# Order of TensorE's work in a chunk-attention loop: where the transposes of xr and the rank products stand

## The chip, the cores and the metric

One core of one Trainium2 chip runs the kernel. The metric is the device time of one execution in microseconds (us). The time before is the median of 3 runs, 677.48 us, the runs lying from 676.41 to 678.26 us.

## What is computed

Two blocks follow each other. The first is attention in chunks of 64 rows, without any link between chunks; the second routes each of the 4608 resulting rows (512 wide) to one of 8 experts by a cosine, and runs that expert's two-layer MLP.

```python
# q, k, v: (8, 8, 576, 64) float32, chunk = 64
scores = scale * q_c @ k_c.T            # 64x64 for each batch, head and chunk
scores = scores - max(scores)
attn = exp(scores); attn = attn / (sum(attn) + 1e-9)
x = (attn @ v_c)  -> rows of all heads: (4608, 512)
xn = x / (norm(x) + 1e-6); en = expert_emb / (norm(expert_emb) + 1e-6)
logits = xn @ en.T / tau                # 8 experts
e = argmax(logits); gate = softmax(logits)[e]
out = gate * (relu(x @ w1[e]) @ w2[e])  # w1: 8x512x1024, w2: 8x1024x512
```

## The kernel before

The 4608 rows are cut into NT = 36 tiles of 128 rows; one tile holds two chunks of all 8 heads. The loop of line 1024, `for t in range(-3, NT + 3)`, is a software pipeline over the tiles, and the order in which it calls its helpers is the order of each engine's queue: the schedule is written by hand (`tc.manual_schedule()`), nothing reorders it. A pass of the loop is called a turn here. In turn t the kernel works on several tiles at once:

- `turn_a(t)` (line 633) transposes the weights a of tile t, four 128x128 transposes on TensorE (L637) into a PSUM tile `tr`, and ScalarE copies them out as aT (L639).
- `turn_qk(t + 3)` (line 590) transposes k and then q of the tile three ahead (L595, four transposes each); ScalarE copies k out (L598), VectorE copies q out (L600). The loads of tile t + 7 (`load_qk`, GpSimd's queue) stand behind it.
- `logits(b)` (line 689), once in four turns, multiplies the transposed rows of a batch of RB = 4 tiles with the experts (L695); ScalarE copies the result (L703). `copy_logits(b)` (line 708) transposes it back on TensorE (L710), and VectorE copies it (L712).
- `scores(t + 2)` (line 603) issues sixteen 64x64 matmuls (L611); VectorE takes the maximum of them (mx, L619) and subtracts it (a, L621). `weights(t + 2)` (line 629) is ScalarE's exp (L631), later in the turn.
- `turn_x(t - 1)` (line 676) transposes the finished rows xr of the tile before (L680); ScalarE copies them out as xT (L682) and sums their squares (L685).
- `values(t)` (line 642) issues sixteen 64x65 matmuls with v (L651); VectorE divides by the sums of the weights: rs (L659), its reciprocal (L660), and the product that writes xr (L662). v of the next batch entry is loaded behind it (`load_v`, SyncE's queue, L584).
- `pick(b)` (line 716), late in the turn in which the logits come, finds each row's expert with five small VectorE instructions (L724 to L728, the last writes eqb_all). One turn later `place(b)` (line 732) counts ranks with five or more small bf16 matmuls (L737, L738, L746), the "rank products", and four VectorE instructions (L762 to L771) make the destinations. `put` scatters one tile a turn to DRAM on GpSimd's queue (L800).

All `tr` tiles come from one PSUM pool with three buffers, used in the order a, k, q, xr, a, and so on, so that each waits for the copy-out of the one three before. The scores have one PSUM buffer and the values have one (`ps_s` and `ps_v`, `bufs=1`).

Turns 33 to 38 are the way out: `early_parts` (line 1013) puts the first matmuls of the expert block there. Behind the loop, groups of 64 rows run through their expert's two layers (L342, L413 and others) until the end.

The loop's head before is (line 1024 on, loads and loops at the way out left out):

```python
turn_a(t); count_early(); turn_qk(t + 3); logits; [turn_x(t - 1) if t == NT]
early_parts(t, 0); scores(t + 2); copy_logits; place
[turn_x(t - 1) if t - 1 < NT - 1]; values(t); load_v
weights(t + 2); pick; put; early_parts(t, 1)
```

Of the kernel before, what the change touches and what calls it, by code (L numbers as in the profile page):

```python
# [25 lines left out]
def kernel(  # L26
# [19 lines left out]
    NT = N // P  # L46
# [77 lines left out]
    def load_first(buf, rows):  # L124

        for s in range(2):
            e = (0, E - 1)[s]
            nc.sync.dma_start(out=whole(buf[s]), in_=rows[:, e : e + 1, :], max_dma_last_dim=4096)
# [317 lines left out]
    with (  # L446
# [132 lines left out]
        def load_v(b, c0=0, c1=NCB, eng=nc.sync):  # L579

            t = v_sb[b % 2]
            for h in range(H):
                r0 = CH * (h % 2)
                eng.dma_start(  # L584
                    out=t[r0 : r0 + CH, h // 2, c0:c1, 0:Dh],
                    in_=v[b, h].rearrange("(c k) d -> k c d", k=CH)[:, c0:c1],
                )
            v_t[b] = t

        def turn_qk(t):  # L590
            for nm in ("kx", "qx"):
                a = qk_t.pop((nm, t))
                ps = ps_t.tile([P, NPAIR, P], FP32, tag="tr", name="tr")
                for i in range(NPAIR):
                    nc.tensor.transpose(ps[:, i], a[:, i * P : i * P + P], ident)  # L595
                x = wk.tile([P, NPAIR, P], FP32, tag=nm + "T", name=nm + "T")
                if nm == "kx":
                    nc.scalar.copy(x, ps)  # L598
                else:
                    nc.vector.tensor_copy(x, ps)  # L600
                qkT[nm, t] = x
# [31 lines left out]
        def turn_a(t):  # L633
            d = st[t]
            ps = ps_t.tile([P, NPAIR, P], FP32, tag="tr", name="tr")
            for i in range(NPAIR):
                nc.tensor.transpose(ps[:, i], d["a"][:, i].rearrange("p r k -> p (r k)"), ident)  # L637
            aT = wk.tile([P, NPAIR, P], FP32, tag="aT", name="aT")
            nc.scalar.copy(aT, ps)  # L639
            d["aT"] = aT  # L640
# [35 lines left out]
        def turn_x(t):  # L676
            d = st[t]
            ps = ps_t.tile([P, KD, P], FP32, tag="tr", name="tr")
            for c in range(KD):
                nc.tensor.transpose(ps[:, c], d["x"][:, c * P : c * P + P], ident)  # L680
            xT = wk.tile([P, KD, P], FP32, tag="xT", name="xT", bufs=RB + 1)
            nc.scalar.copy(xT, ps)  # L682
            d["xT"] = xT
            junk = one.tile([P, D], FP32, tag="junk", name="junk")
            nc.scalar.activation(  # L685
                junk, d["x"], AF.Square, accum_out=xr[:, t % NX, D + SQ : D + SQ + 1]
            )

        def logits(b):

            t = sum(sizes[:b])
            xT = [st.pop(t + i)["xT"] for i in range(RB)]
            for c in range(KD):
                for i in range(RB):
                    nc.tensor.matmul(  # L695
                        lq_ps[Q * i : Q * i + Q],
                        lhsT=enT[:, c],
                        rhs=xT[i][:, c],
                        start=(c == 0),
                        stop=(c == KD - 1),  # L700
                    )
            lq = wk.tile([P, P], FP32, tag="lq", name="lq", bufs=1)
            nc.scalar.copy(lq, lq_ps)  # L703
            copied[b] = lq
# [27 lines left out]
        def place(b):  # L732

            n, t = sizes[b], sum(sizes[:b])
            NE = [P, n, E]
            rank = rt_ps[:, 2, 0:n]
            nc.tensor.matmul(rank, lhsT=sltb, rhs=eqb[:, t : t + n], start=True, stop=False)  # L737
            nc.tensor.matmul(  # L738
                rank,
                lhsT=onesb,  # L740
                rhs=before.unsqueeze(1).to_broadcast(NE),
                start=False,
                stop=n == 1,
            )
            for i in range(n - 1):
                nc.tensor.matmul(  # L746
                    rank[:, i + 1 : n],
                    lhsT=onesb,
                    rhs=eqb[:, t + i].unsqueeze(1).to_broadcast([P, n - 1 - i, E]),
                    start=False,  # L750
                    stop=i == n - 2,
                )
            if b == len(sizes) - 1:
                tot = rt_ps[:, 3, 0]
                nc.tensor.matmul(tot, lhsT=onesb, rhs=before, start=True, stop=False)
                for i in range(n):
                    nc.tensor.matmul(
                        tot, lhsT=onesb, rhs=eqb[:, t + i], start=False, stop=i == n - 1
                    )
            w = wk.tile([P, RB, E], FP32, tag="w", name="w")[:, 0:n]  # L760
            dest = wk.tile([P, RB], I32, tag="dest", name="dest", bufs=3)
            nc.vector.tensor_tensor(w, rank, e_base.unsqueeze(1).to_broadcast(NE), ALU.add)  # L762
            nc.vector.tensor_tensor(w, w, eqb[:, t : t + n], ALU.mult)
            with nc.allow_low_precision("whole numbers"):
                nc.vector.tensor_reduce(dest[:, 0:n], w, axis=AX.X, op=ALU.add)  # L765
            if t + n < NT:
                with nc.allow_low_precision("whole numbers up to 36 + 128"):
                    if n == 1:
                        nc.vector.tensor_tensor(before, before, eqb[:, t], ALU.add)
                    else:  # L770
                        nc.vector.tensor_reduce(  # L771
                            before,
                            eqb_all[:, 0 : t + n + 1].rearrange("p s e -> p e s"),
                            axis=AX.X,
                            op=ALU.add,
                        )
            to_put.extend((dest[:, i : i + 1], xr[:, (t + i) % NX]) for i in range(n))
# [3 lines left out]
        def count_early():  # L781

            cnt = rt_ps[:, 3, 0]
            nc.tensor.matmul(cnt, lhsT=onesb, rhs=before, start=True, stop=True)

            nc.vector.tensor_scalar(full, cnt, -1.0, lim, ALU.mult, ALU.add)
            nc.vector.tensor_scalar(full, full, 0.0, float(P), ALU.max, ALU.min)
            with nc.allow_low_precision("whole numbers up to 36 + 128"):
                nc.vector.tensor_tensor(eqb_all[:, 0], full, ends_e, ALU.mult)
                nc.vector.tensor_tensor(before, before, eqb_all[:, 0], ALU.add)  # L790
# [232 lines left out]
        ends = {sum(sizes[: b + 1]) - 1: b for b in range(len(sizes))}  # L1023
        for t in range(-3, NT + 3):

            if 0 <= t < NT:
                turn_a(t)
            if t == early_t - 1:
                count_early()
            if t + 3 < NT:  # L1030
                turn_qk(t + 3)
                if t + 7 < NT:
                    load_qk(t + 7)
            if t - 2 in ends:
                logits(ends[t - 2])
            if t == NT:
                turn_x(t - 1)
            early_parts(t, 0)
            if 0 <= t + 2 < NT:
                scores(t + 2)  # L1040
            if t - 2 in ends:
                copy_logits(ends[t - 2])
            if t - 3 in ends:
                place(ends[t - 3])
            if 0 <= t - 1 < NT - 1:
                turn_x(t - 1)
            if 0 <= t < NT:
                values(t)
                b = (2 * t + 2) // NCB + 1
                if b not in v_t and b < B and t > 1:  # L1050
                    load_v(b)
            if t == NT - 8:
                load_first(w1_sb, w1_rows)
            if t == NT - 6:
                load_first([w[0] for w in w2_sb], w2_rows)
            if 0 <= t + 2 < NT:
                weights(t + 2)
            if t - 2 in ends:
                pick(ends[t - 2])
            if early_t <= t < early_t + XBUF:  # L1060
                load_early(t - early_t)

            put(1 if t < NT - 2 else 2)
            if t == NT - 3:
                turn_xb(0)
                load_early(XBUF)
            if t == NT - 1:
                turn_xb(1)
            early_parts(t, 1)
            if t == -2:  # L1070
                turn_experts()
            if t == 0:
                constants()
            if t == 1:
                clear_first()
# [151 lines left out]
```

## Time and profile before

| what | value |
|---|---|
| median of 3 runs | 677.48 us |
| the profiled execution, its own time | 673.1 us |
| its span | 671.3 us |
| mean granted TensorE clock | 0.983 |
| TensorE matmul (PE) busy | 623.0 us, 93% |
| VectorE (DVE) busy | 421.3 us, 63% |
| ScalarE (ACT) busy | 443.8 us, 66% |
| GpSimd (POOL) busy | 155.3 us, 23% |
| from 40 to 160 us: PE / DVE / ACT busy | 111.67 / 101.64 / 81.85 of 120 us |
| from 160 us to the end: PE / DVE / ACT busy | 485.73 / 299.41 / 341.87 of 511.3 us |
| the transposes of xr (L680) | 144, first at 18.8 us, last at 165.3 us |
| the rank products (L737) | 9, one for each batch of four tiles |

The attention loop fills about the first quarter of the span (the last transposes of xr start at 165.3 us); the experts fill the rest. The lines shown in the prediction are to be read so: a line of the timeline has its start and its duration in us, the engine, the line of the kernel and the instruction, and in brackets the idle time of that engine just before, with what ended it. A line of the waits says which engine stood before which line, waiting for what: total us, times, longest us.

### The profile page before, as it was taken

To read this page: it belongs to the slowest core of one execution; us is meant where nothing else is said; L and a number is where in the kernel's file an instruction comes from. 1 tells how busy PE (TensorE), PEld (TensorE's weight loads), DVE (VectorE), ACT (ScalarE), POOL (GpSimd) and SP (SyncE) were. 2 spreads that over 40 slices of the span, in tenths; PEclk is the share of its full clock that TensorE was granted. 3 is DMA by queue.
4 is the path that set the end of the run, shared out by engine and by line. 5 is a ranking of instruction groups with operands and counts; after the bars stand their busy time and mean duration, and the time that the engine had idled before them with its cause. 6 is when DMAs were issued, how large, how long until landed. Compare 5 with 4: busy or idle time off the path is not lost. (4 is left out here: it accounts for less than half of the span.)

```text
span 671.3 us, 24844 instructions
## 1 busy us (share of the span) xinstructions
PE 623.0 (93%) x9744; PEld 346.2 (52%) x9744; DVE 421.3 (63%) x1140; ACT 443.8 (66%) x776; POOL 155.3 (23%) x237
## 2 busy tenths in 40 slices
PE   6869998998898989999999999999999999999993
PEld 5658787885443446666434444334444444444431
DVE  4738888986598536547675566757655666565430
ACT  5627776775225847777777867778777677877740
POOL 8827787843310100010000100010001000100101
PEclk9969999999999989999999999999999999999997
DMA  9978999989818711113786111777811115411111
GB/s 256 275 180 233 275 288 269 275 246 371 330 55 300 285 45 35 50 34 111 290 305 210 50 42 43 290 274 253 327 52 50 38 47 167 166 43 34 50 31 35
DMA packets 94590, 112.66 MB, mean 168 GB/s; under 512 B 52364, under 2 KB 72588, under 8 KB 94456
## 3 DMA queue, kind: packets, MB, share of 16 engines
q1 hardware_dynamic: 82728, 72.84, 34.1%
q0 software_dynamic: 11696, 38.04, 17.0%
q8 instruction: 81, 1.33, 0.8%
q14 instruction: 53, 0.43, 0.2%
q10 hardware_dynamic: 32, 0.02, 0.0%
HBM read 334.71 MB, written 22.69 MB: 532 GB/s over the span
## 5 line engine op out<-in xcount | busy, mean ns | idle before, releaser
L413 PE MATMUL y_ps<-w,hT 128*32 128x512 f32 (+1 forms) x2368 | 273.2, 589 | 3.1 <-DVEq L299 3.1
L361 ACT ACTIVATE h<-C 64x256 f32<-64x256 f32 x264 | 178.6, 676 | 95.5 <-DVE C L374 68.9
L413 PEld LDWEIGHTS y_ps<-w,hT 128*32 128x32 f32 x2368 | 93.2, 110 | 153.6 <-issue 123.8
L428 POOL DMA_INDIRECT out_dram<-y,spot x36 | 34.9, 968 | 437.0 <-ACT C L377 198.0
L374 DVE TENSOR_TENSOR C<-C,h 128x256 f32<-128x256 f32 x231 | 96.1, 416 | 49.2 <-DVEq L299 42.5
L342 PE MATMUL h<-w,S 128*32 128x256 f32 x1056 | 98.1, 379 | 1.8 <-DVE w L291 1.8
L342 PE MATMUL h<-sums,xbT 128*32 128x256 f32 x1056 | 97.0, 379 | 0.0
L342 PE MATMUL h<-w,xbT 128*32 128x256 f32 x1056 | 79.4, 380 | 7.0 <-ACTq L299 5.8
L368 DVE STREAM_TRANSPOSE hT<-h 128x512 f32<-128x512 f32 x66 | 46.7, 708 | 44.1 <-ACT h L361 44.0
L342 PEld LDWEIGHTS h<-w,xbT 128*32 128x32 f32 x1056 | 40.8, 110 | 43.2 <-ACTq L299 13.5
L342 PEld LDWEIGHTS h<-w,S 128*32 128x32 f32 x1056 | 49.2, 110 | 24.4 <-DVE w L291 1.5
L342 PEld LDWEIGHTS h<-sums,xbT 128*32 128x32 f32 x1056 | 48.9, 110 | 21.9 <-ACT C L377 0.4
L227 DVE TENSOR_SCALAR rn<-rn 128x1 f32<-128x1 f32 x37 | 5.7, 153 | 72.1 <-ACT rn L224 72.1
L342 PE MATMUL h<-sums,S 128*32 128x256 f32 x528 | 48.7, 379 | 0.0
L800 POOL DMA_INDIRECT spots<-xr,dest x36 | 37.1, 1029 | 35.0 <-DVE dest L765 10.1
L203 DVE STREAM_TRANSPOSE xbT<-xin 128x256 f32<-128x256 f32 x73 | 44.4, 646 | 0.5 <-DVE hT L368 0.5
L224 ACT ACT_TABLE_LOAD x34 | 43.6, 1283 | 0.9 <-issue 0.4
L421 ACT ACTIVATE y<-y_ps,gate 128x512 f32<-128x512 f32 (+1 forms) x37 | 25.2, 682 | 28.6 <-issue 14.7
L231 ACT ACT_TABLE_LOAD x34 | 43.6, 1283 | 0.6
L682 ACT COPY xT<-tr 128x512 f32<-128x512 f32 x36 | 21.1, 586 | 34.2 <-PE tr L680 34.2
L651 PE MATMUL pv<-v,aT 64*64 64x65 f32 x1152 | 28.1, 226 | 9.0 <-DMA v<-in_v_dram 7.4
L572 POOL DMA_DIRECT2D kx<-in_k_dram x36 | 31.5, 876 | 16.4 <-PE tr L595 16.1
(202 smaller groups left out, 800.4 us busy)
## 6 DMA issues: line engine op xcount, KB each, us to landing
w<-in_moe_w_dram SPq DMA_DIRECT2D x74, 2048.0 KB
next_w<-in_moe_w_dram SPq DMA_DIRECT2D x67, 2048.0 KB
xin<-spots SPq DMA_DIRECT2D x158, 64.0 KB
qx<-in_q_dram POOLq DMA_DIRECT2D x32, 256.0 KB, 7.7
v<-in_v_dram SPq DMA_DIRECT2D x56, 144.0 KB
kx<-in_k_dram POOLq DMA_DIRECT2D x28, 256.0 KB, 5.7
spot<-spots SPq DMA_DIRECT2D x80, 4.0 KB
spots<-blank SPq DMA_DIRECT2D x2, 576.0 KB
```

What stands on the lines that cost most here:

```text
L203: nc.vector.transpose(xT[:, :, cols].rearrange("p c (b i) -> p b c i", i=Q), t[:, s * (D // 2) : (s + 1) * (D // 2)].rearrange("p (b i c) ...
L224: nc.scalar.activation(rn, spot[:, j % SPOTS, SQ : SQ + 1], AF.Sqrt)
L231: nc.scalar.activation(sh, sh, AF.Exp, accum_out=gate)
L342: nc.tensor.matmul(ps[t0 : t0 + Q], lhsT=a[:, c, s], rhs=w[:, r], start=c == 0, stop=c == KD // 2 - 1,)
L361: nc.scalar.activation(h[b][G * v : G * v + G, s].rearrange("p (k i) -> p k i", i=Q), x[G * s : G * s + G].rearrange("p (i k) -> p k i", i=Q),
L368: nc.vector.transpose(hT.rearrange("p k (s b i) -> p b s k i", b=2, i=Q)[:, b], h[b].rearrange("p s (k i) -> p s k i", i=Q),)
L374: nc.vector.tensor_tensor(out, a, b, op)
L413: nc.tensor.matmul(ps[Q * r : Q * r + Q, 0:w], lhsT=d["hT"][:, c, Q * t0 : Q * t0 + Q], rhs=w2_sb[s][buf_of(j)][:, c, d0 : d0 + w], start= ...
L428: ins = nc.gpsimd.indirect_dma_start(out=to, out_offset=bass.IndirectOffsetOnAxis(ap=at, axis=0), in_=y[:, 0:w], in_offset=None, bounds_ch ...
L572: eng.dma_start(out=x[done : done + n], in_=src[b, :, s : s + n, :].rearrange("h p d -> p h d"),)
L651: nc.tensor.matmul(pv[CH * c : CH * c + CH, par, i], lhsT=d["aT"][r0 : r0 + CH, i, CH * c : CH * c + CH], rhs=v_t[b][r0 : r0 + CH, i, cb, ...
L800: ins = nc.gpsimd.indirect_dma_start(out=spots, out_offset=bass.IndirectOffsetOnAxis(ap=at, axis=0), in_=m, in_offset=None, bounds_check=S ...
```

## The change

Two calls move, and a condition is merged. `turn_x(t - 1)` moves from behind the scores to a place right behind `turn_qk`, for all tiles; before, only the last tile's stood there. `logits` moves from behind `turn_qk` to a place right behind `turn_a`. `place` moves from before the transposes of xr to behind `values` and the load of v. Nothing is added or removed: TensorE's queue has the same instructions in another order, and so have ScalarE's and VectorE's where those instructions have a consumer. On VectorE the four instructions of `place` now stand behind the three of `values`; on ScalarE the copy of the logits (L703) now stands ahead of that of k (L598).

```diff
             if 0 <= t < NT:
                 turn_a(t)
+            if t - 2 in ends:
+                logits(ends[t - 2])
             if t == early_t - 1:
                 count_early()
             if t + 3 < NT:
                 turn_qk(t + 3)
                 if t + 7 < NT:
                     load_qk(t + 7)
-            if t - 2 in ends:
-                logits(ends[t - 2])
-            if t == NT:
+            if 0 <= t - 1 < NT:
                 turn_x(t - 1)
             early_parts(t, 0)
             if 0 <= t + 2 < NT:
                 scores(t + 2)
             if t - 2 in ends:
                 copy_logits(ends[t - 2])
-            if t - 3 in ends:
-                place(ends[t - 3])
-            if 0 <= t - 1 < NT - 1:
-                turn_x(t - 1)
             if 0 <= t < NT:
                 values(t)
                 b = (2 * t + 2) // NCB + 1
                 if b not in v_t and b < B and t > 1:
                     load_v(b)
+            if t - 3 in ends:
+                place(ends[t - 3])
```

## The prediction

> **What bounds the kernel now.** I began with the page's busy shares and the windows, which say where TensorE (PE) has room, and then read the timeline of the attention loop, because only that loop's order changes. Two windows of four turns each, from one transposition behind the logits' turn to the next:
>
> ```profile
> span 671.3 us, 24844 instructions
> PE 623.0 (93%) x9744; PEld 346.2 (52%) x9744; DVE 421.3 (63%) x1140; ACT 443.8 (66%) x776; POOL 155.3 (23%) x237
> ...
> 46.17:61.36 15.19, 14.52 (x360) 12.42 (x359) 13.29 (x35) 11.08 (x25) 11.21 (x16) 1.00 0.55 159
> 76.92:92.22 15.30, 14.53 (x360) 12.43 (x359) 13.45 (x35) 11.07 (x25) 11.94 (x18) 1.00 1.02 274
> ```
>
> The columns behind the window and its length are PE, PE's weight loads, DVE, ACT and POOL, then PE's clock. Four turns take about 15.2 us, of which PE works 14.5: PE's own queue is the bound of the loop, with DVE (13.3) not far behind. The timeline of PE shows one plain turn:
>
> ```profile
> 53.09 0.63 PE L680 MATMUL tr<-ident,xr 128*128 128x128 f32 x4 [0.27 <-DVE xr L662]
> 53.64 0.70 PE L651 MATMUL pv<-v,aT 64*64 64x65 f32 x32
> 54.27 0.66 PE L637 MATMUL tr<-ident,a 128*128 128x128 f32 x4
> 54.76 0.60 PE L595 MATMUL tr<-ident,kx 128*128 128x128 f32 x4
> 55.20 0.60 PE L595 MATMUL tr<-ident,qx 128*128 128x128 f32 x4
> 55.73 0.69 PE L611 MATMUL sc<-kxT,qxT 64*64 64x64 f32 x32
> 56.35 0.66 PE L680 MATMUL tr<-ident,xr 128*128 128x128 f32 x4
> 56.94 0.69 PE L651 MATMUL pv<-v,aT 64*64 64x65 f32 x32
> ```
>
> From the values at 53.64 to the next at 56.94 are 3.30 us without a gap. The reader should see what stands between a tile's values and the transposes of that tile's xr: a, k, q and the scores of a later tile, 54.27 to 56.35. While PE does those scores, DVE finishes xr. Next, how long DVE and ACT need when they start from fresh scores (their timelines, in two turns where they really waited):
>
> ```profile
> 60.81 0.69 DVE L619 TENSOR_REDUCE mx<-sc 128x8 f32<-128x512 f32 x1 [0.99 <-PE sc L611]
> 61.60 0.69 DVE L621 TENSOR_TENSOR a<-sc,mx 128x512 f32<-128x512 f32 x1
> 62.21 0.18 DVE L712 COPY xr<-rt_ps 128x32 f32<-128x32 f32 x1
> 62.31 0.16 DVE L659 TENSOR_SCALAR rs<-pv 128x8 f32<-128x8 f32 x1
> 62.50 0.20 DVE L660 RECIPROCAL rs<-rs 128x8 f32<-128x8 f32 x1
> 62.74 0.69 DVE L662 TENSOR_TENSOR xr<-pv,rs 128x512 f32<-128x512 f32 x1
> ...
> 70.08 0.63 ACT L631 ACTIVATE a<-a 128x512 f32<-128x512 f32 x1
> 70.61 0.57 ACT L639 COPY aT<-tr 128x512 f32<-128x512 f32 x1
> ```
>
> DVE's queue has mx and a of tile t+2 ahead of rs and xr of tile t, in both kernels. Last, PE's waits from 40 to 160 us:
>
> ```profile
> PE rt_ps L737 <- DVE eqb_all L728: 4.1, 8, 1.8
> PE tr L680 <- ACT kxT L598: 1.4, 3, 0.6
> PE tr L680 <- DVE xr L662: 1.2, 3, 0.6
> ```
>
> Only 4.1 us go to the rank products and 2.6 to xr, the most that an order without waits could win back there.
>
> **The change, part by part.** *Rank products behind the values.* Their wait (4.1 us in all, 1.83 of it the last, at 157.60) goes away as a wait of its own: the values, 0.62, and the xr transposes, 0.56, run first. But see below: in the loop PE will then wait elsewhere, and the saving counts only once, in turn 34. DVE's four instructions of `place` (51.13 to 51.82, 0.69 us) go behind xr instead of ahead of it, which also helps xr in that turn. GpSimd's scatter waits for them and so leaves later within its turn, by about the 1.1 us of rs, reciprocal and xr (51.82 to 52.85 is 1.03); its order against the loads of k and q does not change, and a tile's slot of xr is written again only two turns later, so I put this at nothing.
>
> *Transposes of xr ahead of the scores.* PE itself gains: a turn loses one change between small and full matmuls. Transposes follow transposes every 0.44 us (54.76 to 55.20), but the step from q to the scores is 0.53 and from xr to the values 0.59. New steps: values .63, a .49, k .44, q .44, xr .55 (as 53.09 to 53.64), scores .62, in all 3.17 instead of 3.30. The step from scores straight to values is not in this trace in a running turn; I bound it by 0.53 and 0.63 and take 0.62, as scores to xr.
>
> The Trainium skill (TensorEngine Tiling, Key Properties) says that a change of the tiling mode drains TensorE. The steps of 0.53 and 0.59 against 0.44 agree; if that alone decided, the loop would be 0.13 us a turn faster, about 4 us over 29 turns, instead of slower as below.
>
> But the order closes a loop. The new queue is values(t-1), a, k, q, xr(t-1), scores(t+2), values(t). The transposes of xr(t-1) wait for DVE's xr(t-1), and everything behind them waits too, first the scores that DVE needs for its next mx. In DVE's queue xr(t) stands behind that mx and a. So from one transposition of xr to the next there is a chain that no overlap hides, all from rows:
> - xr transposes start to scores start: 0.55 (53.09 to 53.64)
> - scores start to mx start: 0.77 (the scores before 60.81 start at 60.04)
> - mx to a: 0.79; a to rs: 0.60 (54.17 to 54.77, a turn without L712); rs to reciprocal 0.19; reciprocal to xr 0.24
> - xr start to PE's xr transposes: 0.84 (DVE's xr of that turn starts at 52.25, PE at 53.09)
>
> Sum: 3.98 us a turn. A second chain runs over ACT, because xr's PSUM buffer is freed by the copy of aT, which stands behind exp in ACT's queue: 0.55 + 0.77 + 0.79, a to exp 0.73 (69.35 to 70.08), exp to aT 0.53, aT itself 0.57, ACT's end to PE 0.05 (162.06 to 162.11): 3.99. Both give 4.0 us. PE's 3.17 lies inside, with 0.8 to spare, so the 0.13 saved is hidden by the wait; without the wait it would be worth the 4 us above.
>
> The Trainium skill (TensorE: Matmul & The Clock Gate, Part 3) says that matmuls start and end strictly in program order, only weight loads being pulled ahead. The waits at L680 above, with the values idle behind them, agree; could PE have passed the blocked transposes, the sum would be the 3.17 a turn.
>
> *What lies on top in some turns.* Logits now stand between a and k; with 1.01 (137.56 to 138.57) PE's steps from one xr to the next are 4.18, 0.18 over the chain; I take 0.2, seven times: 1.4. The copy L712 adds 0.10 ahead of rs, eight times: 0.8. `pick`, 1.06 (48.15 to 49.21), and the copy of q, 0.60, stand between xr and the next mx: xr 0.61 + 1.06 + 0.60 = 2.27 against 0.84 + 0.55 + 0.77 = 2.16 in the chain, 0.11, seven times: 0.8. One stop of PE inside the scores, 1.2 at 107 us ("issue", waiting for nothing shown), stays. Together 4.2. `place` with the copy of q, 0.61 + 0.69 + 0.60, fits in 2.16 and costs nothing until its last reduction grows (0.66 at 159.06).
>
> *The sum.* Until about 40 us nothing counts: PE stands 5.6 us before v in turn 4 (to 38.29 us), and the new loop reaches that stand only about 1 us later. Behind it PE runs the same steps in turn 5; xr(4) of the new order starts where the scores start now, 44.85. Then 29 chains to xr(33): 44.85 + 29 x 4.0 + 4.2 = 165.1. Today xr(33) starts at 157.72, so 7.4 later; behind it stand xr .55, values .63 and rank .13 before the first early matmuls, 1.31 against 1.19 now: 7.5. From there order and waits are as before, and what follows hangs on the attention's rows, so it shifts whole. Loads of the first weights and rows are issued from the loop's turns and shift with it.
>
> The profiled execution has a span of 671.3 and a time of 673.1, which is 4.4 below the median of 677.48. Its new time would be 680.6; on the median I predict 677.48 + 7.5 = **685.0 us**, 1.1% slower. Ends: with the chain at 3.91 (mx to a at 0.72, as in 53.45 to 54.17) and only the 1.2 on top, 44.85 + 113.4 + 1.2 + 1.3 = 160.8 against 158.91 now, +1.9; with a chain of 4.08 (0.05 of late start at both hand-overs between engines) and 5.5 on top (`place` then costing 0.2 in each group), +11. I take 679.5 to 690.
>
> **The rivals.** *Faster, PE stays the bound.* If xr is ready when PE comes, a turn is 3.17: 0.13 x 29 = 3.8, and the rank waits of 4.1 go too: 8 less, 669.5. For it: 93% PE, and the L737 waits are real. Against: it needs the chain under 3.3, while mx, a, rs, reciprocal and xr on DVE alone take 0.79 + 0.60 + 0.19 + 0.24 + 0.69 = 2.5 from fresh scores, and xr and scores add 1.2 before. It decides from the point where the chain is under 3.87, today's mean of a turn ((157.72 - 45.64) / 29). Chance 0.09.
>
> *No change to be seen.* The chain is 3.85 to 3.9, so that what it costs equals the waits it swallows; that needs the latencies between engines to shrink by 0.1 where queues are already blocked: 677.5. Or the loop is held by transfers (DMA share 1.02 above) whatever PE does; against that, no wait of PE behind 40 us names a DMA. Chance 0.08.
>
> *Much slower, the clock falls.* With 0.8 us idle in each 4.0 the granted clock drops as it did behind the 5.6 us stand, where the window 40.37 to 46.17 has a clock of 0.63 and transposes take 1.06 instead of 0.60. Then xr and scores add about 0.9 a turn, 26 in all: 711. Against: the windows of 20 us from 160 and from 220 us have 17.3 and 16.9 us of PE work and clocks of 1.00 and 0.98. Chance 0.04.
>
> **How the numbers follow.** The forecast has 0.79. 0.3%, 2 us, is about what a measurement can tell from no change. The range leaves out the faster rival, most of the unchanged one and the clock, 0.2 in all. Faster 0.09, same 0.08, slower 0.83.
>
> **What would show it.** In the profile of the changed kernel: starts of L680 4.0 us apart in plain turns; PE idle before L680 of about 0.8 a turn, 20 to 25 us in all, laid to DVE's xr or to ACT; no wait at L737 in the loop; windows of four turns at 16.5 us with PE 14 of it; the last L680 near 173 instead of 165.3; the experts' part as long as now. Distances of 3.2 to 3.4 with no wait at L680 would prove it wrong, and so would an experts' part that takes the delay back.

## The result and the profile after

The changed kernel takes 687.6 us (median of 4 runs, 686.45 to 688.81) against 677.45 for the kernel before beside it: a ratio of 1.0151, interval 1.0127 to 1.0175. Forecast were 685.0 us and a range of 679.5 to 690. First the page's head and two windows of four turns each; the columns behind the window's length are PE, weight loads, DVE, ACT, POOL, PE's clock, DMA share, GB/s.

```profile
span 685.3 us, 24851 instructions
PE 622.4 (91%) x9744; PEld 345.2 (50%) x9744; DVE 421.8 (62%) x1140; ACT 447.0 (65%) x776; POOL 155.4 (23%) x237
...
67.13:85.98 18.85, 14.64 (x359) 12.31 (x359) 13.61 (x35) 11.68 (x26) 12.22 (x17) 1.00 0.82 240
85.98:102.31 16.33, 14.40 (x359) 12.22 (x359) 13.47 (x35) 11.37 (x26) 11.86 (x18) 1.00 0.94 249
```

PE's work is the same to 0.6 us. Undisturbed groups of four turns take 16.3 to 16.7 us instead of 15.2 to 15.6, with 14.3 to 14.6 us of PE in them. The first of the two shown has 2.5 us more on top, to which I come back. Then the timelines of PE, DVE and ACT in one plain turn of the changed kernel:

```profile
89.94 0.66 PE L680 MATMUL tr<-ident,xr 128*128 128x128 f32 x4 [0.66 <-ACT aT L639]
90.52 0.69 PE L611 MATMUL sc<-kxT,qxT 64*64 64x64 f32 x32
91.04 0.76 PE L651 MATMUL pv<-v,aT 64*64 64x65 f32 x32
91.73 0.66 PE L637 MATMUL tr<-ident,a 128*128 128x128 f32 x4
92.22 0.60 PE L595 MATMUL tr<-ident,kx 128*128 128x128 f32 x4
92.66 0.60 PE L595 MATMUL tr<-ident,qx 128*128 128x128 f32 x4
94.03 0.33 PE L680 MATMUL tr<-ident,xr 128*128 128x128 f32 x1 [0.78 <-ACT aT L639]
```

```profile
91.43 0.69 DVE L619 TENSOR_REDUCE mx<-sc 128x8 f32<-128x512 f32 x1 [0.26 <-PE sc L611]
92.15 0.69 DVE L621 TENSOR_TENSOR a<-sc,mx 128x512 f32<-128x512 f32 x1
92.76 0.15 DVE L659 TENSOR_SCALAR rs<-pv 128x8 f32<-128x8 f32 x1
92.95 0.20 DVE L660 RECIPROCAL rs<-rs 128x8 f32<-128x8 f32 x1
93.19 0.69 DVE L662 TENSOR_TENSOR xr<-pv,rs 128x512 f32<-128x512 f32 x1
```

```profile
92.88 0.63 ACT L631 ACTIVATE a<-a 128x512 f32<-128x512 f32 x1 [1.04 <-DVE a L621]
93.41 0.57 ACT L639 COPY aT<-tr 128x512 f32<-128x512 f32 x1
```

Read it round: PE starts xr at 89.94 and the scores at 90.52; DVE starts from the scores at 91.43, a at 92.15; ACT's exp at 92.88, aT at 93.41 to 93.98; PE's next xr at 94.03, 4.09 us after the last. DVE's branch ends at 93.88 and, with the 0.15 it takes to PE, at the same 94.03. PE had q's transposes out at about 93.25 and stood 0.78 us. Last, PE's waits from 0 to 240 us:

```profile
PE tr L680 <- ACT aT L639: 12.4, 17, 1.1
PE pv L651 <- DMA v<-in_v_dram: 6.6, 3, 5.5
PE pv L651 <- issue: 4.8, 3, 2.1
PE tr L680 <- DVE lmax L724: 4.7, 8, 1.4
...
PE rt_ps L737 <- DVE eqb_all L728: 1.4, 1, 1.4
```

The rank products wait no more inside the loop (the one wait left is on the way out); 17.5 us now stand before L680, 14.8 of them in the 29 turns that the experiments measure.

### The profile page after: what moved, and what is told of

The parts are those of the page before. It is cut to its first block, busy times and chain, and to the rows that moved or that the text cites. A ratio compares the mean times of both kernels' runs of the same rounds, so it can differ in the third digit from the quotient of the medians.

```text
span 685.3 us, 24851 instructions
## 1 busy us (share of the span) xinstructions
PE 622.4 (91%) x9744; PEld 345.2 (50%) x9744; DVE 421.8 (62%) x1140; ACT 447.0 (65%) x776; POOL 155.4 (23%) x237
## 3 DMA queue, kind: packets, MB, share of 16 engines
q0 software_dynamic: 11696, 38.04, 16.7%
## 5 line engine op out<-in xcount | busy, mean ns | idle before, releaser
L413 PE MATMUL y_ps<-w,hT 128*32 128x512 f32 (+1 forms) x2368 | 274.5, 591 | 3.3 <-DMA w<-in_moe_w_dram 3.3
L413 PEld LDWEIGHTS y_ps<-w,hT 128*32 128x32 f32 x2368 | 93.7, 111 | 154.6 <-issue 125.2
L631 ACT ACTIVATE a<-a 128x512 f32<-128x512 f32 x36 | 22.7, 630 | 37.6 <-DVE a L621 37.6
L680 PE MATMUL tr<-ident,xr 128*128 128x128 f32 x144 | 22.9, 281 | 17.5 <-ACT aT L639 12.4
```

The lines of the kernel that those rows point to most:

```text
L413: nc.tensor.matmul(ps[Q * r : Q * r + Q, 0:w], lhsT=d["hT"][:, c, Q * t0 : Q * t0 + Q], rhs=w2_sb[s][buf_of(j)][:, c, d0 : d0 + w], start= ...
```

## The experiments

Eleven edits and a second run of the kernel before. In all of them I use one measure besides the time: the loop, from the start of xr(4)'s transposes (turn 5) to that of xr(33)'s (turn 34), 29 turns, read from PE's timeline. The last two columns are its mean turn and the shortest of the four turns in its usual groups: in the kernel before one turn in four is as short as 3.27 us, the others take 3.6 to 4.5.

| kernel | time, us | before beside it | ratio (95%) | loop, us | mean turn, us | shortest turn, us |
|---|---|---|---|---|---|---|
| before | 677.45 | | | 112.1 | 3.87 | 3.27 |
| changed | 687.6 | 677.45 | 1.0151 (1.0127 to 1.0175) | 123.7 | 4.26 | 3.96 |
| e1 xr back behind the scores | 677.66 | 675.66 | 1.0039 (1.0007 to 1.0071) | 113.0 | 3.90 | 3.24 |
| e2 xr alone moved | 690.74 | 675.66 | 1.0216 (1.0180 to 1.0253) | 127.0 | 4.38 | 3.93 |
| e3 exp behind aT | 685.75 | 675.66 | 1.0142 (1.0109 to 1.0176) | 125.1 | 4.31 | 3.92 |
| e4 values first, exp behind aT | 687.72 | 675.66 | 1.0160 (1.0118 to 1.0203) | 123.0 | 4.24 | 3.10 |
| e5 place alone moved | 684.82 | 686.28 | 0.9986 (0.9948 to 1.0023) | 117.6 | 4.05 | 3.24 |
| e6 logits alone moved | 683.12 | 686.28 | 0.9966 (0.9933 to 0.9999) | 114.1 | 3.93 | 3.5 |
| e7 values first | 719.0 | 686.28 | 1.0475 (1.0406 to 1.0544) | 152.1 | 5.24 | 4.80 |
| e8 values first, next tile's exp | 690.9 | 686.28 | 1.0066 (1.0037 to 1.0095) | 126.7 | 4.37 | 3.80 |
| e9 the same, exp behind k | 689.93 | 688.86 | 1.0013 (0.9979 to 1.0047) | 124.6 | 4.30 | 3.10 |
| e10 changed, maximum twice | 711.21 | 688.86 | 1.0322 (1.0286 to 1.0357) | 146.2 | 5.04 | 4.7 |
| e11 before, maximum twice | 694.05 | 688.86 | 1.0077 (1.0047 to 1.0108) | 131.4 | 4.53 | 3.69 |
| e12 before again | 677.62 | 675.54 | 1.0022 (0.9979 to 1.0065) | 112.0 | 3.86 | 3.27 |

The kernel before took 676 us beside e1 to e4 and e12, and 686 to 689 beside e5 to e11: chips differ by more than the change is worth, so only ratios, and turns within one profile, are compared. For e5 to e11 the profiles come from chips of the slower kind as well, from which there is none of the kernel before or of the changed one, and the changed kernel's 1.0151 was measured beside a kernel before of 677 us.

**e1: xr back.**

```diff
-            if 0 <= t - 1 < NT:
+            if t == NT:
                 turn_x(t - 1)
 ...
                 copy_logits(ends[t - 2])
+            if 0 <= t - 1 < NT - 1:
+                turn_x(t - 1)
```

> The changed kernel with the transposes of xr put back behind the scores; logits and place stay where the change put them. Theory (a chain through DVE and ACT closed by xr's place): the chain opens, turns return to 3.3 us, the waits at L737 stay away, so 673 to 677.5 us, at or a little under the time before. Rival (the early logits or the late place cost the time): 684 us or more.

677.66 us, ratio 1.0039: the shortest turns are 3.24 us and the loop 113.0, so the chain is gone with xr's place alone. Against the expectation it is not under the time before: it lies 0.2 us over the range, and its interval leaves it 0.1 to 0.7% slower. DVE's queue shows why nothing is won (timelines of e1 behind a turn with logits, PE last):

```profile
65.35 0.19 DVE L728 TENSOR_TENSOR eqb_all<-sel,pm 128x32 bf16<-128x32 f32 x1
65.46 0.68 DVE L600 COPY qxT<-tr 128x512 f32<-128x512 f32 x1
...
68.08 0.69 DVE L662 TENSOR_TENSOR xr<-pv,rs 128x512 f32<-128x512 f32 x1 [0.30 <-DMA spots<-xr,dest]
...
68.92 0.63 PE L680 MATMUL tr<-ident,xr 128*128 128x128 f32 x4 [0.67 <-DVE w L762]
```

The wait at L737 was DVE's backlog behind `pick`. With the rank products out of the way PE runs into the same backlog at the next xr (0.67; the name w is of the instruction that DVE had begun by then, xr ends at 68.77). Over the loop PE waits 5.6 us before L680 in e1, where the kernel before has 4.1 before L737 and 2.6 before L680. Part of the 0.67 is new: VectorE itself waits 0.30 until the scatter's DMA has fetched the rows that xr overwrites, 5.3 us in eight turns of e1's loop. It comes with the late `place`, behind which the scatter is late too: e5, with `place` alone moved, has 5.0 us of it, e2 and e6, where it stays early, none, and the kernel before 0 and 0.6 in its two profiles. The prediction put this term at nothing; in the changed kernel it is 0.6 us, once.

**e2: only xr moved.**

```diff
-            if t == NT:
+            if 0 <= t - 1 < NT:
                 turn_x(t - 1)
 ...
-            if 0 <= t - 1 < NT - 1:
-                turn_x(t - 1)
```

> The kernel before with only the transposes of xr moved ahead of the scores; logits and place as before. Theory: the chain is closed by this alone, L680 starts about 4.05 us apart in plain turns, 684 to 690 us. Rival (the three moves must act together, or logits and place cost it): within 2 us of 677.5.

690.74 us, just over the expected range, ratio 1.0216. The move of xr alone makes the whole loss and more: with `place` still ahead of the values, its four VectorE instructions stand inside the chain. From xr(5) to xr(6) are 4.70 us (50.41 to 55.11), in the changed kernel 4.03 (50.75 to 54.78): 0.67 more, near the 0.69 that the four took in the trace of before; in the six groups behind, the same turn takes 4.69 to 4.97 in e2. So the late `place` of the change softens its own loss.

**e3: ACT's branch opened.** `weights` of the tile after next is called one turn later, right behind `turn_a`.

```diff
                 turn_a(t)
+            if 0 <= t + 1 < NT:
+                weights(t + 1)
 ...
-            if 0 <= t + 2 < NT:
-                weights(t + 2)
```

> The changed kernel with ScalarE's exp (L631) called one turn later, behind the copy of aT, so that the copy no longer stands behind exp; everything else as changed. Theory (two chains of the same length, 3.98 over DVE and 3.99 over ACT): DVE's chain still holds, turns of 3.95 to 4.0 us, 0 to 3 us less than the changed kernel, 684 to 688. Rival (only the chain over ACT decides, as the profile's waits for aT suggest): turns near 3.3, 668 to 676 us.

685.75 us, a ratio of 1.0142 against 1.0151: no difference that the intervals show, within the 0 to 3 us expected and far from the rival's 668 to 676. Turns without logits mostly take 3.92 to 4.09 us. PE's waits of e3:

```profile
PE tr L680 <- DVE w L762: 4.4, 7, 0.7
PE tr L680 <- DVE lmax L724: 4.2, 7, 1.4
...
PE tr L680 <- ACT kxT L598: 3.4, 4, 0.9
```

The changed kernel's 12.4 us "for aT" are gone as a name, the waiting is not: with one branch open the other, as long, holds the loop. A wait's name says who came last, not what would be won without it.

**e7: the other branch opened, the first left.** I tell it here, out of order. Values come ahead of scores, so that DVE has xr(t) ahead of mx(t+2); exp stays.

```diff
-            if 0 <= t + 2 < NT:
-                scores(t + 2)
-            if t - 2 in ends:
-                copy_logits(ends[t - 2])
             if 0 <= t < NT:
                 values(t)
 ...
                     load_v(b)
+            if 0 <= t + 2 < NT:
+                scores(t + 2)
+            if t - 2 in ends:
+                copy_logits(ends[t - 2])
```

> The changed kernel with values(t) ahead of scores(t+2), ScalarE's exp left where it was. Theory: DVE's chain opens, but the chain over ACT grows: values start to rs 0.77, rs to xr 0.43, xr to mx 0.61, mx to a 0.75, a to exp 0.73, exp to aT 0.53, aT to PE 0.62, xr to values 0.56, in all 5.0 us a turn instead of 4.06; 29 turns, 27 us more than the changed kernel, 702 to 718 us. Rival (a wait laid to aT is only a name for DVE's lateness): 680 to 690.

719.0 us, 1.0475 of before, on the chip where before took 686.28; that is 1 us over the expected range, which counted from the faster kind of chip. The loop's distances are what tells: of four turns two are mostly 4.8 to 5.0 us where the sum said 5.0, the one with logits has 5.06, and the one behind it, with `pick` in VectorE's queue, mostly 5.6 to 5.8. Two turns on PE:

```profile
92.78 0.66 PE L680 MATMUL tr<-ident,xr 128*128 128x128 f32 x4 [1.89 <-ACT aT L639]
93.36 0.70 PE L651 MATMUL pv<-v,aT 64*64 64x65 f32 x32
93.88 0.80 PE L611 MATMUL sc<-kxT,qxT 64*64 64x64 f32 x32
...
94.77 1.09 PE L637 MATMUL tr<-ident,a 128*128 128x128 f32 x4
95.66 1.06 PE L595 MATMUL tr<-ident,kx 128*128 128x128 f32 x4
96.51 1.06 PE L595 MATMUL tr<-ident,qx 128*128 128x128 f32 x4
97.77 0.66 PE L680 MATMUL tr<-ident,xr 128*128 128x128 f32 x4 [0.20 <-ACT aT L639]
```

From 92.78 to 97.77 are 4.99 us, in which exp stands on DVE's a, and aT behind exp. Note the idle time of only 0.20 before the second: PE's granted clock was 0.50 from 94.70 to 97.60, and the transposes of a, k and q, 1.06 to 1.09 us long instead of 0.60 to 0.66, filled the wait. The turn did not get longer. In a chain that PE does not decide, slower PE work costs nothing until it fills the wait.

**e4, e8, e9: both branches opened, xr still behind q.** All have e7's order on PE. e4 has e3's exp; e8 calls `weights(t + 1)` where `weights(t + 2)` stood; e9 calls it behind `turn_qk`:

```diff
                 if t + 7 < NT:
                     load_qk(t + 7)
+            if 0 <= t + 1 < NT:
+                weights(t + 1)
```

> As e3, and values(t) are issued ahead of scores(t+2), so that on DVE rs and xr of tile t stand ahead of mx and a of tile t+2: both chains open, xr stays behind k and q. Theory: PE's steps are 0.56 + 0.52 + 0.62 + 0.49 + 0.44 + 0.44 = 3.07 a plain turn, DVE 3.05; with the extras of a group of four DVE needs 13.9 us, 3.5 a turn instead of 3.87 before, 29 turns: about 11 us less than before, 664 to 671 us. Rival (the place of xr behind q costs by itself, whatever DVE and ACT do): 684 or more.

> As e7, but the exp at the end of a turn is that of tile t+1, whose a is a turn old, so that neither the copy of aT nor that of k waits behind it. Theory: both chains open and DVE's 13.9 us a group of four become the bound; with rests of waits 14.2 to 15.0 us a group, 667 to 675 us. Rival (as e4 came out: values ahead of scores loses whatever it opens): 683 or more.

> As e8, with the exp of tile t+1 between ScalarE's copies of k and of xT, so that neither aT nor the transposes of the next a wait behind it (in e8 they did, 13.9 us at L637). Theory: the chains are open; left are DVE's 13.9 us a group of four and the waits of L662 for the scatter's DMA that e8 had (13 us in all); 14.5 to 15.5 us a group, 0.990 to 1.002 of before. Rival (xr behind q loses by itself): 1.010 of before or more.

e4 missed: 1.0160 where 664 to 671 us was expected. The shortest turn of its groups is 3.1 us, PE's own steps, so the chain did open there, but its groups are 15.3 us and more, and its mean turn, 4.24, is the changed kernel's. e8 missed too, 1.0066, while e9 met its range at 1.0013. PE's waits of e8 and DVE's waits of e8 and of e9 name what PE and DVE wait for in place of the chain:

```profile
PE tr L637 <- ACT a L631: 13.9, 24, 1.4
...
PE rt_ps L737 <- DVE eqb_all L728: 2.9, 5, 1.4
```

```profile
DVE xr L662 <- DMA spots<-xr,dest: 13.0, 8, 5.0
```

```profile
DVE xr L662 <- DMA spots<-xr,dest: 8.9, 9, 3.4
```

In e8 exp stands behind ACT's copy of xT and its squares, and the next a behind exp: a third chain, which I had not drawn. e9 frees it (0.8 us left at L637), but its loop is only 2.1 us shorter, so that this chain held e8's loop is not shown. What remains in e9 is DVE waiting to overwrite a slot of xr whose rows the scatter's DMA has not fetched yet (e4 has 14.7 us of this in its loop), the rank products waiting for `pick` again, and 6.3 us in its loop in which PE stops for nothing shown. Which of these holds e4 or e9 no run decides. By its ratio e9 takes no longer than before beside it, with xr where the change put it; so that place need not cost the 1.5%. But its loop, 124.6 us, is as long as the changed kernel's, what the loop of before was on that chip is not on record, and e4, with the same order on PE, lost 1.6% on a chip of the faster kind. Nor does the order win anything here.

**e5, e6: the other two moves alone.** In the kernel before, `place` behind the load of v (e5), or `logits` behind `turn_a` (e6), each as the change has it.

```diff
-            if t - 3 in ends:
-                place(ends[t - 3])
 ...
                     load_v(b)
+            if t - 3 in ends:
+                place(ends[t - 3])
```

> The kernel before with only place (the rank products) moved behind the values. Theory: the wait at L737 is DVE's backlog behind pick; taken from there it shows again a turn later at the transposes of xr, so 0 to 2 us less than before. Rival: the 4.1 us of waits at L737 are saved, 3 to 5 us less than before.

> The kernel before with only logits moved ahead of k and q. Theory: PE's instructions and the chains are the same; the copy of k on ScalarE and q on VectorE come 1 us later in one turn of four; within 2 us of before, rather above. Rival: the early logits cost more than 3 us.

0.9986 and 0.9966. e5 is within the 2 us expected. e6 is 2.3 us less by its ratio, just outside them and on the other side than expected; its interval, 0.9933 to 0.9999, hardly leaves 1, so I call neither faster. The 4.1 us of waits at L737 do not come back as time when `place` moves: in e5's loop none is left there, and 7.8 us stand before L680 instead. The ends of e5's interval, 3.6 us less and 1.6 more, do not quite exclude the rival's 3 to 5.

**e10, e11: a known piece more on DVE.** The maximum of the scores (L619) is issued twice, in the changed kernel and in the one before; the outputs stay what they are. Lines behind it count one more.

```diff
             nc.vector.tensor_reduce(mx, sc, axis=AX.X, op=ALU.max)
+            nc.vector.tensor_reduce(mx, sc, axis=AX.X, op=ALU.max)
```

> The changed kernel with VectorE's maximum of the scores (L619) done twice. Theory: the maximum lies in the closed chain, so each of 29 turns is longer by its 0.71 to 0.72, about 20 us more than the changed kernel, 1.040 to 1.050 of before. Rival (the loop is held elsewhere, by DMA or instruction supply): less than 8 us more.

> The kernel before with the maximum of the scores done twice. Theory: there DVE has 13.8 us of a group's 15.4; with 2.9 more it becomes the bound at 16.7, 1.3 a group, about 9 us more than before in all (7 to 13 us, 1.010 to 1.019). Rival (the chain is closed there too): 20 us, 1.030.

On the same chip the extra instruction leaves 1.0322 for the changed order and 1.0077 for the one before: 17 us apart (711.21 - 694.05) where the kernels without it are 10 apart (on their chip). The sizes are smaller than expected: 1.0322 is 0.017 above the changed kernel's ratio, about 12 us and not 20, and 1.0077 is 5 us and not 7 to 13. The turns grow by more. In e10 two of a group's plain turns are mostly 4.6 to 4.9 us, 0.7 to 0.8 longer than the changed kernel's, so the instruction goes into them in full; the third is 5.2 or more, at least 1.1 longer. In e11 the shortest turn of a group is 3.69 instead of 3.27, about DVE's instructions end to end (2.99 as in the trace of before, plus 0.72), but its first group takes 17.45 us instead of 15.19, 2.3 more where 1.3 were expected. The loops are 22.5 us longer in e10 and 19.3 in e11 than in the first profiles of their kernels. So the pair does not by itself tell the closed chain from a VectorE queue that is nearly full; e1, e2, e3 and e7 do that. Why the totals show less than the loops I could not settle, for there is no profile of the unchanged kernels from that chip. There the loop of before may itself have been longer by stops of PE, which a waiting turn hides.

**e12: the kernel before once more.**

> The kernel before, unchanged, for a second profile of it, since chips differ: its median was 676 us beside e1 to e4 and 686 to 689 beside e5 to e11, where the profiles show PE stopped for nothing shown (issue) behind the loop. Theory: where it takes 685 us or more, its first L413 comes 31 to 35 us after the loop's last turn instead of 23, and its plain turns stay 3.27 us, so that the chip's share is not a chain; on a chip of the other kind it repeats the first profile, 112 us for 29 turns and 23 behind. Rival: plain turns of the kernel before reach 4 us there too, and the closed chain would not be the change's doing.

It landed on a chip of the first kind, at 677.62 us, and repeats the first profile nearly turn for turn: a loop of 112.0 us, shortest turns of 3.27, 24 us from xr(33) to the first L413. What the kernel before does in the loop on the other kind of chip stays open.

## Why the prediction was right, step by step

**The closed chain** was the step that carried the forecast, and it holds: 4.0 us was the sum, 3.96 to 4.09 the distance in most turns without logits or a stop (four have 4.18 to 4.37, which no run explains). Its links in the turn shown: xr to scores 0.58 (0.55 taken), scores to mx 0.91 (0.77), mx to a 0.72 (0.79), a to exp 0.73, exp to aT 0.53, aT 0.57, to PE 0.05, in all 4.09. Two links were off, by 0.14 and by 0.07 the other way, and partly cancel. e2 and e1 show that xr's place alone closes and opens it; e3, that DVE's branch alone holds the turn; e7, that the one over ACT does, at the 5.0 computed for it; that the two are nearly equal is read from the turn shown. e10 agrees: a link made 0.7 longer makes turns 0.7 longer.

**What lies on top.** For a group of four the steps gave 16.0 + 0.2 (logits) + 0.1 (L712) + 0.1 (`pick`) = 16.4; the four undisturbed groups have 16.3, 16.4, 16.6 and 16.7. Logits turns are 4.15 to 4.21 for 4.18 to 4.20. The turn behind `pick` takes 3.96, so its 0.11 did not appear.

**The stops of PE were mis-sized.** I let "one stop of PE, 1.2 us" stand. In this profile the loop has three, two of them in the group of 18.85 us, and 0.85 us of waiting at the count of L784, where before had none:

```profile
72.19 0.29 PE L651 MATMUL pv<-v,aT 64*64 64x65 f32 x6
74.62 0.68 PE L651 MATMUL pv<-v,aT 64*64 64x65 f32 x26 [2.14 <-issue]
...
78.85 0.64 PE L695 MATMUL rt_ps<-xT,enT 128*32 128x128 f32 x16
80.41 0.64 PE L695 MATMUL rt_ps<-xT,enT 128*32 128x128 f32 x16 [0.92 <-issue]
```

PE stops in the middle of sixteen values and of the logits, where no wait stands in the code. The turns that hold these four are 5.52, 5.31, 5.19 and 5.26 us instead of 4.09 and 4.21, together 4.6 longer. That is 3.4 more than the 1.2 I let stand, and the loop is 123.7 where the steps gave 120.2. From 46 to 165 us the changed kernel, e3, e4 and e9 have 4.3 to 5.4 us of such stops, all other profiles 0.5 to 1.9. They are not all chance of an execution. The stop that I let stand comes again in e12, with the same length and behind the same matmul (the kernel before, then e12, whose lines count one more):

```profile
106.19 0.50 PE L611 MATMUL sc<-kxT,qxT 64*64 64x64 f32 x17
107.88 0.46 PE L611 MATMUL sc<-kxT,qxT 64*64 64x64 f32 x15 [1.19 <-issue]
...
106.83 0.50 PE L612 MATMUL sc<-kxT,qxT 64*64 64x64 f32 x17
108.52 0.46 PE L612 MATMUL sc<-kxT,qxT 64*64 64x64 f32 x15 [1.19 <-issue]
```

So this one goes with the program, and a new order may well move or add stops. How an order does that is not shown.

**Before 46 us.** v for turn 4 landed at 42.09, not at 38.29 as in the trace of before, and xr(4) started at 46.69 and not at 44.85: 1.8 us. This is no work of the change as far as is known: the kernel before, in e12, has v at 40.43 and its own xr(4) at 46.72 instead of 45.64. With the 3.4 that makes the 5.3 us by which xr(33) came later (170.35) than computed (165.1); the last L680 starts at 177.50, not near 173.

**The two clocks of comparison.** The profiles are 14.0 us apart in span, the medians 10.15. I had set the sum against a profiled execution that lay 4.4 us under its median; the changed one's lies 0.5 under. So the loop's longer stops stand in the profile, and the median sees 2.7 us more than the 7.5 forecast. That it came so near is in part luck. At the first early matmuls, where the sum ends, the profile of the changed kernel is 12.9 us later (171.81 against 158.91) where 7.5 were computed; 3.9 of the 14.0 us between the profiles are only that the first one of before was fast for its kernel.

**Smaller points.** PE stands 14.8 us before L680 in the loop, not 20 to 25: in one turn of four the logits fill the wait, and in the next only 0.4 to 0.5 are left of it. The step from scores to values is 0.51 to 0.52 in running turns (90.52 to 91.04), under my lower bound of 0.53; it lies under the wait and costs nothing. The Trainium skill (TensorEngine Tiling, Key Properties) has a drain at each change of tiling mode, and these numbers agree: scores and values share a mode, while from scores to transposes of xr it was 0.62. The first L413 starts 11.85 us later, 1.05 less than the early matmuls; behind it the experts take 492.5 us instead of 490.3. On the whole nothing was taken back, as forecast; the 2.2 more I did not pursue.

**The rivals.** PE as the bound (faster) needed a chain under 3.87 us; it is 3.96 to 4.09. No change fell with it. The clock stayed at 1.00 in all windows of the loop behind 46 us, with 0.4 to 1.1 us idle in each plain turn.

## What to carry to other kernels

Moving an instruction earlier in one in-order queue can close a ring through the others: write down the ring (this wait, what is queued behind it, who needs that, back to what is waited for) and add its links before counting saved steps. Compare the ring with the mean turn, not with the engine's work; here 4.0 against 3.87 decided it although PE was 93% busy. A wait that moves away from one instruction and comes back at the next, as in e1 and e5, is not that instruction's: it is a backlog of the engine it waits for.

## What the runs showed of the hardware that was not expected

PE stops inside a run of matmuls without a wait in the code: in the changed kernel three times in the loop, for 0.9 to 2.1 us, in other loops 2 to 14 times, for 0.2 to 2.4 us. One such stop, 1.19 us, came at the same matmul in both profiles of the kernel before. PE's granted clock fell to 0.50 in e7 (94.70 to 97.60) although the longest idle stretch of PE in its loop until then was 1.9 us; in the changed kernel, with stretches up to 2.1 us in the loop, it stayed at 1.00. On the chips beside which the kernel before took 686 to 689 us, PE was also served in drops behind the loop; from e11's timeline of PE:

```profile
207.28 0.42 PE L253 MATMUL h_ps<-w,xbT 128*32 128x256 f32 x2 [0.36 <-issue]
208.04 0.38 PE L253 MATMUL h_ps<-w,xbT 128*32 128x256 f32 x1 [0.34 <-issue]
208.75 1.02 PE L253 MATMUL h_ps<-w,xbT 128*32 128x256 f32 x2 [0.34 <-issue]
```

A few matmuls every 0.75 us, where the kernel before has 64 in 3.66 us in its first profile. From xr(33) to the first L413 it takes 31 to 35 us in e5 to e11, and 22 to 24 in all other profiles. No engine or DMA is named for it; that instructions come late is my reading, not shown.
